# FNet mixing and a quick-GELU block on one core: another order of j for the first transfers, rounding of the weights moved behind the copies, one weight row turned by a transfer, output in runs of 256 bytes with the last group in halves

One core of a Trainium2 chip. The metric is the device time of one launch in microseconds (us); lower is better. PE is the matrix engine (TensorE), DVE VectorE, ACT ScalarE, POOL GpSimd and SP SyncE; loads and stores are issued by SP and ACT, each on a queue of its own. "pa", "psw" and the like are the kernel's names for PSUM banks, and groups of instructions are called by them.

## The reference, cut to what matters

```python
def reference(x, w_in, w_out):            # x 8 x 3008 x 256, w_in 256 x 2048, w_out 2048 x 256
    X = np.fft.fft(np.fft.fft(x, axis=1), axis=2).real.astype(np.float32)
    h = X.reshape(8 * 3008, 256) @ w_in
    g = h * (1.0 / (1.0 + np.exp(-1.702 * h)))
    return (g @ w_out).astype(np.float32)
```

## The kernel before

The FFT over 3008 = 47 x 64 rows is done in two stages of matmuls, with symmetric rows folded on each other first. Between the stages the data goes through DRAM: `spill` writes it to Td, `fill` reads it back. The FFT over 256 columns is folded into w_in (`fold_w`, PSUM name psw; the result is wcs). The weights come as pairs of 32-bit words and are rounded by the kernel, in eight chunks (four of w_in, four of w_out): `bounds` is one operation on POOL (m) and three on ACT (g, r, r), `rounded` three on DVE (m, a, a) and one add on POOL (wst or wo). The long part is 384 steps: `hidden` (pa, pb), `rows` (DVE), `activate` (ACT), `product` (po). For the first sequence all of the preparation stands on the way:

```python
    nc.scalar.dma_start(out=w0, in_=tab1[:, 0:n0 + 1])
    load_first(0, 4, nc.sync)
    load_first(4, 4, nc.scalar)
    load_first(8, 8, nc.sync)
    nc.scalar.dma_start(out=small[:], in_=tab2)
    load_in(0, nc.scalar)
    load_in(1, nc.sync)
    load_out(0, nc.sync)
    warm(10)                                   # matmuls on ones, to keep the clock up
    ...
    for k in range(8):
        if k < 7:
            fold_first(k + 1)
        else:
            bounds(("in", 0))                  # ACT: 3 operations ahead of the last copy
        mix_first(k)                           # 8 matmuls and one copy out of PSUM on ACT
        if k % 4 == 3:
            spill(0, 2 * k - 6, 2 * k + 2, (nc.sync, nc.scalar if k == 7 else nc.sync))
    fill(0, 0, 4)
    round_in(0)
    finish_in(0)
    warm(4)
    bounds(("in", 1))
    fold_w(0)
    fill(0, 4, NG)
    load_out(1, nc.sync)
    rotate(0, 0, 4, nc.scalar.copy)
    stage2(0, 0)
    round_in(1)
    ...                                        # cut
    def nyquist_weights(n):                    # row 0 of wcs[1] turned into a column by matmuls
        ps = bank("psa")
        for f in range(4 * n, 4 * n + 4):
            nc.tensor.matmul(ps[:, f:f + 1], lhsT=wcs[1][0:1, f * 128:(f + 1) * 128], rhs=ones[:, 0:1],
                             start=True, stop=True)
        nc.scalar.activation(af2[:, 4 * n:4 * n + 4], ps[:, 4 * n:4 * n + 4], ACTF.Copy, scale=2.0)
```

Of the kernel before, what the change touches and what calls it, by code (L numbers as in the profile page):

```python
# [34 lines left out]
NA, NB = 47, 64  # L35
# [70 lines left out]
def kernel(ctx: ExitStack, tc, x, w_in, w_out, tab1, tab2, out):  # L106
# [20 lines left out]
    Xr = [nc.dram_tensor(f"Xr{b}", (NA, NJ - 1, D), F32, kind="Internal").ap() for b in range(B)]  # L127
# [27 lines left out]
    def turn(b):  # L155

        for m0, m1 in ((NJ + 1, NJ + 17), (NJ + 17, NB)):
            n = m1 - m0
            nc.sync.dma_start(out=view(Xr[b], (m0 - NJ - 1) * D, [D, n], [(NJ - 1) * D, NA], [1, D]),
                              in_=view(x[b], ((NA - 1) * NB + m0) * D, [D, n], [-NB * D, NA], [1, D]))  # L160

    def load_x(b):

        for r in range(2):
            for p0, p1 in PIECES:
                t, src = xt[64 * r + p0:64 * r + p1], x[b].rearrange("(p j) d -> p j d", j=NB)[p0:p1]
                rev = Xr[b][p0:p1]
                both = [16 * D, 2], [1, 8 * D]
                nc.sync.dma_start(out=t[:, 0:16, :].rearrange("p (c i) d -> p c (i d)", c=2), in_=free(src, 8 * r * D, *both))

                if r:
                    nc.sync.dma_start(out=t[:, 16:32, :].rearrange("p (c i) d -> p c (i d)", c=2),
                                      in_=free(rev, (8 - 8 * r) * D, *both))
                    continue
                nc.sync.dma_start(out=t[:, 16:24, :], in_=rev[:, 8:16, :])
                nc.sync.dma_start(out=t[:, 24:31, :], in_=rev[:, 24:31, :])
                nc.sync.dma_start(out=t[:, 31, :], in_=src[:, NJ, :])
# [24 lines left out]
    def mix1(b, m):  # L202

        ps = [bank("ps1") for _ in range(2)]
        for i in (2 * m, 2 * m + 1):
            for r in range(2):
                for c in range(2):
                    rows, o = slice(64 * r, 64 * r + NA), ps[r][64 * c:64 * c + 64, i % 2 * D:(i % 2 + 1) * D]
                    jj = 16 * c + 8 * r + i
                    if jj:  # L210
                        nc.tensor.matmul(o, lhsT=mat(w1, jj, rows), rhs=xt[rows, 31 - (8 * c + i), :], start=True, stop=True)  # L211
                        continue
# [5 lines left out]
        for r in range(2):  # L218
            q = 8 * r + 2 * m
            nc.scalar.copy(xt[:, q:q + 2, :].rearrange("p j d -> p (j d)"), ps[r][:])  # L220
# [5 lines left out]
    def load_first(lo, n, eng):  # L226
        for p0, p1 in PIECES:
            m = p1 - p0
            both = [16 * D, 2], [1, n * D]
            eng.dma_start(out=free(xt[p0:p1], lo * D, *both), in_=view(x, (NB * p0 + lo) * D, [NB * D, m], *both))  # L230
            for c in range(2):
                a = 16 * c + lo
                t, src = xt[NA + p0:NA + p1], NB * p0 * D
                if a == 0:
                    eng.dma_start(out=t[:, 0, :], in_=view(x, src + NJ * D, [NB * D, m], [1, D]))
                z, a = a + n, max(a, 1)
                eng.dma_start(out=t[:, a:z, :], in_=view(x, src + (NB - a) * D, [NB * D, m], [-D, z - a], [1, D]))

    def fold_first(k):

        t, e = xt[0:2 * NA], room[k % 4][0:2 * NA]

        def src(at, *last):
            return free(t, 2 * k * D + at, [16 * D, 2], [D, 2], list(last))

        def dst(at, *last):
            return free(e, at, [2 * D, 2], [D, 2], list(last))

        nc.scalar.copy(dst(0, H, 2), src(0, H, 2))
        for at, op in ((1, ALU.add), (H + 1, ALU.subtract)):  # L250
            nc.vector.tensor_tensor(dst(at, 1, H - 1), src(1, 1, H - 1), src(D - 1, -1, H - 1), op=op)

    def mix_first(k):

        ps, e = bank("ps1"), room[k % 4]
        for i in range(2):
            for even in range(2):
                for c in range(2):
                    jj, (c0, c1) = 16 * c + 2 * k + i, (0, H + 1) if even else (H + 1, D)
                    w, n = (w0o, jj) if jj and not even else (w0, jj or ENDS[1 - even])  # L260
                    nc.tensor.matmul(ps[64 * c:64 * c + 64, i * D + c0:i * D + c1], lhsT=mat(w, n, slice(0, 128)),  # L261
                                     rhs=e[:, 2 * c + i, c0:c1], start=True, stop=True)
# [13 lines left out]
    def spill(b, q0=0, q1=16, engines=(nc.sync, nc.sync)):  # L276

        for c, eng in enumerate(engines):
            eng.dma_start(out=view(Td[b], (16 * c + q0) * D, [NJ * D, NM], [1, (q1 - q0) * D]),
                          in_=xt[64 * c:64 * c + NM, q0:q1, :].rearrange("p q d -> p (q d)"))  # L280
# [51 lines left out]
    def load_out(n, eng):  # L332
        t = raw["out", n] = cv.tile([128, 1024, 2], U32, tag="raw", bufs=3, name="raw")
        eng.dma_start(out=t[:].rearrange("p (f n) w -> p f (n w)", f=4),
                      in_=w_out[4 * n * 128:(4 * n + 4) * 128, :].bitcast(U32).rearrange("(f p) n -> p f n", p=128))
# [21 lines left out]
    def rounded(out, key):  # L357
# [10 lines left out]
        return lambda: nc.gpsimd.tensor_tensor(out.bitcast(U32), a[:], r[:], op=ALU.add)  # L368
# [4 lines left out]
    def round_in(n):  # L373
        wst[n] = op.tile([128, 2, 512], F32, tag="os", name="wst")
        last["in", n] = rounded(wst[n][:].rearrange("p i f -> p (i f)"), ("in", n))

    def round_out(n):
        ps = slice(2 * n, 2 * n + 2)
        last["out", n] = rounded(wo[:, ps].rearrange("p f q n -> p (f q n)"), ("out", n))
# [14 lines left out]
    def fold_w(n):  # L394
        for cs in range(2):
# [3 lines left out]
            nc.scalar.copy(wcs[cs][:, n * 512:(n + 1) * 512], ps[:])  # L399

    def nyquist_weights(n):
        ps = bank("psa")
        for f in range(4 * n, 4 * n + 4):
            nc.tensor.matmul(ps[:, f:f + 1], lhsT=wcs[1][0:1, f * 128:(f + 1) * 128], rhs=ones[:, 0:1],  # L404
                             start=True, stop=True)
        nc.scalar.activation(af2[:, 4 * n:4 * n + 4], ps[:, 4 * n:4 * n + 4], ACTF.Copy, scale=2.0)
# [96 lines left out]
    def combine(t):  # L503
# [5 lines left out]
        o = op.tile([128, 4, 256], F32, tag="os", name="os")  # L509
        if t < NP:  # L510
            for half in range(2):
                nc.vector.transpose(o[:, 2 * half:2 * half + 2, :].rearrange("p i n -> p (i n)"),
                                    pot[half][:].rearrange("p i n -> p (i n)"))
        else:
            c = cv.tile([128, 4, 256], F32, tag="m", name="c")
            if n < 256:
                nc.gpsimd.memset(c[:, :, n:], 0.0)
            (_, m6), (m2, m7), (m5, m3), (m4, _) = ((pot[q][:, 0, :n], pot[q][:, 1, :n]) for q in range(4))
            u2, u3, u4 = (op.tile([128, 256], F32, tag=f"u{q}", bufs=1, name=f"u{q}")[:, :n] for q in (1, 2, 3))
            c1 = pot["c"][:, :n]  # L520
            c11, c12, c21, c22 = (c[:, q, :n] for q in range(4))
            for out_, i0, i1, how in ((u2, c1, m6, ALU.add), (c11, c1, m2, ALU.add), (u3, u2, m7, ALU.add),
                                      (u4, u2, m5, ALU.add), (c12, u4, m3, ALU.add), (c22, u3, m5, ALU.add),
                                      (c21, u3, m4, ALU.subtract)):
                nc.vector.tensor_tensor(out_, i0, i1, op=how)
            for half in range(2):
                nc.vector.transpose(*(x[:, 2 * half:2 * half + 2, :].rearrange("p i n -> p (i n)") for x in (o, c)))
        store(b, blk, hh, o, n)

    def store(b, blk, hh, o, n):  # L530
# [161 lines left out]
```

## Time and profile before

| | before |
|---|---|
| time, median of the runs beside the changed kernel | 1942.39 us |
| span of the profiled run | 1939.2 us |
| first pa (regular work begins) | 49.63 us |
| first step of width 225 ("step 8") | 102.85 us |
| last matmul ends | 1931.08 us |

These four points cut the span into four pieces: the start (to the first pa), the stretch (first pa to step 8, in which the other weight chunks are prepared beside the first eight steps), the steady part (step 8 to PE's last matmul) and the end. They are read from the timeline of PE: the first line with pa, the first pa line of shape 128x225, and the last line. The prediction shows the first and the last of them; this is step 8 (a line of a timeline has: start, length, engine, line of the kernel, operation, result <- operands, shapes, how many in the group, and in brackets the engine's wait ahead of it and what ended it):

```profile
102.85 0.92 PE L429 MATMUL pa<-pq,wcs 128*128 128x225 f32 x4
```

### The profile page before, as it was taken

The page shows a single profiled execution, that of the slowest core. Times are in us where ns is not written, and L with a number is a line of the kernel's source. Part 1 is how long each engine was busy: PE and PEld are TensorE (multiplying, and loading weights), DVE is VectorE, ACT ScalarE, POOL GpSimd, SP SyncE. Part 2 cuts the span into 40 slices and gives each one's busy share as a digit, 9 for nine tenths or more (in the row PEclk, how much of TensorE's full clock was granted, in tenths as well). Part 3 has the DMA queues.
Part 4 walks back from the last instruction along what each step waited for, and adds up shares of the span by engine and source line. Part 5 has one row for each costly group of instructions (what it writes and reads, how often), then busy time and mean ns, then how long its engine had stood idle before and what let it go on. Part 6 is the DMA issues. An engine that isn't in the chain of part 4 may idle for free.

```text
span 1939.2 us, 29813 instructions
## 1 busy us (share of the span) xinstructions
PE 1908.7 (98%) x10730; PEld 1673.0 (86%) x10730; DVE 1409.5 (73%) x2924; ACT 671.6 (35%) x927; POOL 756.3 (39%) x1045
## 2 busy tenths in 40 slices
PE   6999999999999999999999999999999999999998
PEld 3698888988889888898889888898888988889887
DVE  3867777777778767876777677777776777778766
ACT  3633333333333333333333333333333333333332
POOL 1465223642246322463225522254223642223222
PEclk8999999999999999999999999999999999999999
DMA  8820451227202372134521353222721223202201
GB/s 214 219 51 10 87 84 15 48 46 120 17 12 52 52 112 17 16 53 77 81 21 30 55 90 51 25 48 43 109 28 15 17 46 57 18 12 24 19 12 22
DMA packets 242389, 103.11 MB, mean 53 GB/s; under 512 B 207779, under 2 KB 232099, under 8 KB 238982
## 3 DMA queue, kind: packets, MB, share of 16 engines
q1 hardware_dynamic: 238880, 97.53, 32.2%
q10 hardware_dynamic: 3363, 3.69, 0.7%
q8 instruction: 85, 1.39, 0.3%
q14 instruction: 61, 0.50, 0.1%
HBM read 57.91 MB, written 47.67 MB: 54 GB/s over the span
## 4 chain that ended last, share of the span: by engine, by line
PE 96%; DMA 2%; ACT 1%; DVE 0%; SPq 0%; issue 0%; DVEq 0%; ACTq 0%
PE po L496 59%; PE pa L429 17%; PE pb L429 17%; PE ps L211 1%; PE ps L304 1%; DMA xt<-in_x_dram 1%; DMA raw<-in_moe_w_in_dram 1%; PE psw L398 0%; PE ps L215 0%; DMA Td<-xt 0%; PE ps L261 0%; ACT g L346 0%; PE psa L404 0%; ACT wcs L399 0%; ACT r L353 0%
## 5 line engine op out<-in xcount | busy, mean ns | idle before, releaser
L470 POOL TENSOR_TENSOR s<-h 128x256 f32<-128x256 f32 (+1 forms) x376 | 270.3, 719 | 1093.4 <-ACT h L458 1028.5
L496 PE MATMUL po<-s,wt 128*128 128x256 f32 (+1 forms) x2256 | 599.7, 375 | 0.0
L433 ACT COPY v<-pa 128x512 f32<-128x512 f32 (+1 forms) x384 | 222.0, 578 | 1065.1 <-PE pa L429 1065.1
L443 DVE TENSOR_TENSOR h<-v,pb 128x512 f32<-128x512 f32 (+1 forms) x384 | 259.0, 675 | 402.5 <-PE pb L429 395.1
L496 PEld LDWEIGHTS po<-s,wt 128*128 128x128 f32 x2256 | 428.6, 190 | 48.4
L496 PE MATMUL po<-h,wo 128*128 128x256 f32 (+1 forms) x1632 | 469.6, 375 | 0.0
L458 ACT ACTIVATE h<-h 128x1024 f32<-128x1024 f32 (+1 forms) x384 | 400.8, 1044 | 16.9 <-DVE h L453 15.3
L429 PE MATMUL pa<-pq,wcs 128*128 128x256 f32 (+1 forms) x1536 | 394.8, 379 | 1.2 <-DVE pq L310 1.2
L429 PE MATMUL pb<-pq,wcs 128*128 128x256 f32 (+1 forms) x1536 | 388.6, 375 | 0.0
L496 PEld LDWEIGHTS po<-h,wo 128*128 128x128 f32 x1632 | 310.1, 190 | 35.5
L446 DVE SCALAR_TENSOR_TENSOR dif<-nb,af,pb 128x256 f32<-128x256 f32 (+1 forms) x768 | 328.3, 469 | 3.7 <-ACT nb L322 1.9
L429 PEld LDWEIGHTS pa<-pq,wcs 128*128 128x128 f32 x1536 | 286.9, 190 | 48.2 <-issue 9.6
L429 PEld LDWEIGHTS pb<-pq,wcs 128*128 128x128 f32 x1536 | 292.3, 190 | 33.6 <-DVE dif L446 0.3
L471 POOL TENSOR_TENSOR s<-h 128x256 f32<-128x256 f32 (+1 forms) x376 | 276.7, 736 | 0.0
L453 DVE TENSOR_TENSOR h<-pa,dif 128x512 f32<-128x512 f32 (+1 forms) x448 | 265.4, 604 | 13.2
L496 PE MATMUL po<-s,wo 128*128 128x256 f32 (+1 forms) x752 | 220.3, 375 | 0.0
L496 PE MATMUL po<-h,wt 128*128 128x256 f32 (+1 forms) x752 | 220.3, 375 | 0.0
L474 DVE TENSOR_TENSOR s<-h,s 128x256 f32<-128x256 f32 (+1 forms) x376 | 200.7, 534 | 12.9
L473 DVE TENSOR_TENSOR s<-s,h 128x256 f32<-128x256 f32 (+1 forms) x376 | 180.5, 480 | 4.3 <-POOL s L470 4.3
L496 PEld LDWEIGHTS po<-s,wo 128*128 128x128 f32 x752 | 142.9, 190 | 16.1
L496 PEld LDWEIGHTS po<-h,wt 128*128 128x128 f32 x752 | 142.9, 190 | 16.1
L197 POOL TENSOR_TENSOR xt<-xt 111x510 f32<-111x510 f32 x56 | 74.1, 1323 | 4.4
(62 smaller groups left out, 697.8 us busy)
## 6 DMA issues: line engine op xcount, KB each, us to landing
out_dram<-os SPq DMA_DIRECT2D x568, 32.0 KB
Td<-xt SPq DMA_DIRECT2D x14, 768.0 KB
t<-Td SPq DMA_DIRECT2D x7, 1536.0 KB
xt<-in_x_dram SPq DMA_DIRECT2D x15, 512.0 KB
nb<-pq SPq DMA_DIRECT2D x23, 256.0 KB
out_dram<-os SPq DMA_DIRECT2D x192, 28.0 KB
Xr<-in_x_dram SPq DMA_DIRECT2D x7, 752.0 KB
Xr<-in_x_dram SPq DMA_DIRECT2D x7, 705.0 KB
```

The source lines that it names most:

```text
L197: eng.tensor_tensor(low, low, free(t, up + D - 1, [-D, 2], [-1, D - 1]), op=ALU.add)
L429: nc.tensor.matmul(ps[:, i * 256:i * 256 + n], lhsT=wcs[cs][:, f * 128:(f + 1) * 128], rhs=pq[:, cs, ks], start=True, stop=True)
L433: nc.scalar.copy(two(v[:], n), two(pa[:], n))
L443: nc.vector.tensor_tensor(two(h[:], n), two(v[:], n), two(pb[:], n), op=ALU.add)
L446: nc.vector.scalar_tensor_tensor(dif[:, i * 256:i * 256 + n], nb[:, ks], af2[:, f:f + 1], pb[:, i * 256:i * 256 + n], op0=ALU.mult, op1=AL ...
L453: nc.vector.tensor_tensor(free(h[:], 512 + at + m - 1, [256, 2], [RUN, blocks], [-1, m]), *ins, op=ALU.add)
L458: nc.scalar.activation(g, g, ACTF.Gelu_apprx_sigmoid)
L470: eng.tensor_tensor(s1, a21, a22, op=ALU.add)
L471: eng.tensor_tensor(s3, a11, a21, op=ALU.subtract)
L473: eng.tensor_tensor(s2, s1, a11, op=ALU.subtract)
L474: eng.tensor_tensor(s4, a12, s2, op=ALU.subtract)
L496: nc.tensor.matmul(pot[q][:, i, :n], lhsT=lhs, rhs=rhs, start=(p == 0 and i == 0 and f == 0), stop=(p == NP - 1), skip_group_check=True)
```

## The change

The intent: fewer transfers for the first sequence, in an order in which four neighbouring j make one unit of work, with the weights behind them; the last copies out of PSUM ahead of the rounding; no small matmuls to turn one row of the folded weights; half as many output packets and issues, and the last group's first half stored while the second is summed. The diff, cut:

```diff
-    load_first(0, 4, nc.sync)
-    load_first(4, 4, nc.scalar)
-    load_first(8, 8, nc.sync)
+    both = nc.sync, nc.scalar
+    load_first(0, 8, (nc.sync, nc.sync))
+    load_first(8, 20, both)                    # forward rows on SP's queue, reversed rows on ACT's
+    load_first(20, 32, both)
     nc.scalar.dma_start(out=small[:], in_=tab2)
-    load_in(0, nc.scalar)
+    load_in(0, nc.sync)
     load_in(1, nc.sync)
     load_out(0, nc.sync)
-    warm(10)
+    warm(6)
 ...
         if k < 7:
             fold_first(k + 1)
-        else:
-            bounds(("in", 0))
         mix_first(k)
-        if k % 4 == 3:
-            spill(0, 2 * k - 6, 2 * k + 2, (nc.sync, nc.scalar if k == 7 else nc.sync))
+        if k in (3, 5, 7):
+            spill(0, 0 if k == 3 else 2 * k - 2, 2 * k + 2, both if k == 7 else (nc.sync, nc.sync))
     fill(0, 0, 4)
+    bounds(("in", 0))
     round_in(0)
 ...                                            # fold_w: the row, and wcs read with a stride of 4
-    def nyquist_weights(n): ...
+        row = cv.tile([1, 512], F32, tag="e", name="row")
+        nc.scalar.activation(row[:], ps[0:1, :], ACTF.Copy, scale=2.0)
+        nc.scalar.dma_start(out=af2[:, 4 * n:4 * n + 4], in_=row[:])
 ...                                            # round_out: the columns in another order, two adds on POOL
+            return [(free(out, dh * H, [2 * H, 4], [32, 4], [1, 32]),
+                     [free(t, 32 * dh, [2 * H, 4], [64, 4], [1, 32]) for t in ins]) for dh in range(2)]
 ...                                            # the end
+            if t == len(steps) - 1 and out_ is c12:
+                turned(0, c[:])
+        for half in (1,) if t == len(steps) - 1 else (0, 1):
+            turned(half, c[:, 2 * half:])
 ...                                            # store: 4 transfers of 256-byte runs for 8 of 128
-            for i in range(8):
+        for q in range(4):
```

Cut: the other indices of j in the matmuls, `load_x`, `turn`, `spill` (pieces of 1 KB) and `load_out`, which follow from the new orders.

## The prediction

> **What bounds the kernel now.** I read the page first: how busy each engine is, and the 40 slices.
>
> ```profile
> PE 1908.7 (98%) x10730; PEld 1673.0 (86%) x10730; DVE 1409.5 (73%) x2924; ACT 671.6 (35%) x927; POOL 756.3 (39%) x1045
> PE   6999999999999999999999999999999999999998
> DMA  8820451227202372134521353222721223202201
> ```
>
> TensorE works 98% of the span; only its first and last slices are not full. Next the table of busy time by window.
>
> ```profile
> 20.00:30.00 10.00, 2.09 (x26) 1.88 (x24) 2.91 (x5) 1.20 (x4) 1.09 (x1) 0.80 1.07 244
> 70.00:80.00 10.00, 8.43 (x33) 5.74 (x34) 9.65 (x12) 8.00 (x11) 4.31 (x3) 1.00 1.01 306
> 300.00:500.00 200.00, 200.00 (x1170) 176.72 (x1169) 147.90 (x311) 68.60 (x96) 83.44 (x118) 1.00 0.34 55
> 1920.00:1940.00 20.00, 11.09 (x52) 9.42 (x50) 7.27 (x16) 1.43 (x2) 2.73 (x4) 0.85 0.17 27
> ```
>
> Columns: window, its length, busy time of PE, weight load, DVE, ACT and POOL with counts, granted clock, DMA share, GB/s. From 100 to 1920 us every window shows PE busy for all of its length. So nothing done to DMA, DVE, ACT or POOL there can shorten it; what can shrink is the start (0 to 100 us) and the tail. The timeline of PE shows the start.
>
> ```profile
> 15.23 5.38 PE L261 MATMUL ps<-e,wt 128*64 128x127 f32 x64 [2.93 <-issue]
> 28.52 5.80 PE L261 MATMUL ps<-e,wt 128*64 128x127 f32 x64 [7.91 <-DVE e L251]
> 46.98 0.36 PE L291 MATMUL psr<-t,small 128*128 128x4 f32 x2 [2.24 <-DMA t<-Td]
> 49.63 1.85 PE L429 MATMUL pa<-pq,wcs 128*128 128x256 f32 x4 [1.21 <-DVE pq L310]
> 61.33 1.05 PE L404 MATMUL psa<-ones,wcs 1*128 1x1 f32 x8 [0.77 <-ACT wcs L399]
> 70.89 3.70 PE L398 MATMUL psw<-wst,small 128*128 128x512 f32 x8 [1.41 <-DVE h L453]
> ```
>
> Regular work begins at 49.63 us. Before it the transform of the first sequence waits twice for x: PE has nothing from 20.6 to 28.5. Then comes the way through DRAM. The full chain of waits, asked for the first 110 us, gives its length.
>
> ```profile
> 15.93 11.04 DMA xt<-in_x_dram
> 34.11 1.05 ACT g L346
> 37.80 5.02 DMA Td<-xt
> 44.62 11.83 DMA raw<-in_moe_w_in_dram
> ```
>
> The last x transfer was issued at 15.93 and landed at 26.97. ACT then put 3.1 us of rounding of the weights (L346, L353, L354: 34.01 to 37.21 in ACT's timeline) ahead of the last copy out of PSUM, at 37.21; the write to Td could leave only at 37.80. So the start is set by the order of transfers and of ACT's work, not by PE.
>
> The tail, from the timeline of the end:
>
> ```profile
> 1930.49 0.59 PE L496 MATMUL po<-h,wt 128*128 128x256 f32 x2
> 1932.15 1.30 DVE L527 STREAM_TRANSPOSE os<-c 128x512 f32<-128x512 f32 x2
> 1932.88 3.83 SPq L544 DMA_DIRECT2D out_dram<-os  x8
> 1932.88 3.94 ACTq L544 DMA_DIRECT2D out_dram<-os  x8
> ```
>
> PE ends at 1931.1. Eight issues on each of two queues take 3.9 us, 0.48 us each, until 1936.8; the span ends at 1939.2, 2.4 us later.
>
> **What the Trainium skill says.** "DMA: Bandwidth & Descriptors", section "Queues, rings and completion order", says that the queues of SP and ACT are rings on the same 16 engines, served in ring order, with the engine going round-robin between the rings. The trace agrees: in the start DMA is 0.8 to 1.1 busy and a second queue shares the rate. So an earlier x transfer means later weights; the order decides. The same page, "Specifications", gives 512 B as the least size for line rate. The trace has 207,779 of 242,389 packets below that, and yet a DMA share of about a third in the steady part. "TensorE: Matmul & The Clock Gate", section "Part 1: The HAM clock gate (the "warmup" mystery)", says that the array falls to half clock after an idle window of about 3.4 us. The windows of 1 us agree: after the hole before 46.98 the granted clock is 0.50 from 50 to 53 us. I expect that loss to remain.
>
> **The change, part by part.**
>
> *First transfers of x.* Before, each group of folds takes j from two separate halves, so the first half of the work needs two sets of transfers and the second waits for a third, which stands in the queues among the tables and the first weight chunk. After, four neighbouring j belong together, loads are j 0-8, 8-20, 20-32, and the weights come behind. The bytes do not change: x is 3.08 MB, table 0.8 MB. From the windows of 1 us: by 7 us 1.45 MB had moved, 0.65 MB of it x. With only x under way the rate was 181 GB/s (7 to 13.6 us, both queues) and 153 GB/s (22 to 27 us, one queue). The other 2.43 MB of x at 170 GB/s take 14.3 us: x has landed at about 21.5 us instead of 27.0. That saves 5.5 us, but it pushes weights back. Behind x must pass the small table 0.4 MB, three weight chunks of 1.05 MB each and the spills 1.57 MB, before the fill may start. Weights went at about 390 GB/s (27 to 33 us): 3.55 MB take 9.1 us. The spill now has pieces of 1 KB instead of 8 KB. Packets of 1 KB took 46 ns where they ran well and up to twice that elsewhere, so 1536 packets on 16 engines at 55 ns are 5.3 us. Sum: 21.5 + 9.1 + 5.3 = 35.9 us for the end of the spill, 42.8 before. The compute is not behind that: the last three folds (1.25 us of DVE each) and the PE work on them end at about 26.5 us.
>
> *Copies ahead of rounding.* It takes 3.1 us off ACT ahead of the last copy. It is part of the same path: with the old order 26.5 would be 29.6 us, still ahead of the queue. So I do not add it to the sum. The rounding of the first weights (ACT 1.1, DVE 3.1, POOL 2.4) and its fold on PE (3.7) can end by about 37 us, while the fill lands.
>
> *From the fill to regular work.* Fill issued to landed 4.0 us (42.96 to 46.98), landed to the first hidden matmul 2.65 us, neither changed: 35.9 + 4.0 + 2.65 = 42.6, plus 0.5 for issues: 43.1 instead of 49.6. **Gain 6.5 us.**
>
> *One row turned by a transfer.* L404 goes: four groups, 1.13 + 3 x 1.05 = 4.3 us of PE, and 2.1 us that PE waits for the ACT copies ahead of three of them. In their place ACT does one activation of 1x512 (an estimate from its 128x512 copy: 0.6 us) and issues a transfer (about 0.4 us on ACT), which lands about 2 us on. 6.4 us is the most. But between 68.7 and 94.2 us DVE has almost no gap and between 57 and 70 ACT has none; PE waited 1.4 us for DVE at 70.89. Some of what PE saves becomes a wait for them. On the other side weight chunk 2, which held ACT at 56.5 us (6.9 us after regular work began), should come some 2 us earlier relative to it. **Gain 4 us of the 9.7 us** that this stretch (49.63 to 102.85) spends beyond PE's needed 43.5 us (eight hidden steps of 1.73, five products and three folds of 3.45 each, 2 of small things).
>
> *Output.* Runs of 256 B halve the stores' packets, 192,500 to 96,250, and their issues, 16 to 8 per group. In the steady part this saves nothing on PE. At the end the first half is transposed as soon as its two blocks are summed, and its stores leave under the rest of the sums. After the second transpose (still about 1933.5) two issues per queue are left: 0.96 us, then the 2.4 us. 1933.5 + 3.4 = 1936.9 instead of 1939.2. **Gain 2.3 us.**
>
> *Steady part.* Loads in 2 KB pieces, spills in 1 KB pieces, POOL adds in two halves, transposes with another stride: all beside a PE that never waits. **0 us.** Sum: 6.5 + 4 + 2.3 = 12.8 us; 1942.9 - 12.8 = 1930.1.
>
> **Rivals.** First, x is bound by how its rows are read, not by order: the packets from x ran at half the rate of others (153 GB/s alone). Then longer first transfers on both queues might fall below 150 GB/s, x lands near 24 us, and three chunks of weights are still behind it: only some 3 us of the first term come, total about 1934. Against it: with both queues on x the rate was the higher one. Second, ACT and DVE become the bound at 57 to 94 us: the row, its transfer and strided PSUM reads take more than PE's 4.3 us give. Then the second term is 0 and the sum 8.8: 1934. For it: the full timelines of both. Third, the weights arrive early enough for both to run ahead, and all of the 6.4 us plus the late chunk's wait fall away, with x at 19 us: 6.5 + 2.5 + 8 + 2.3 gives 1923.5. Fourth, a store or fold blocks PE in the steady part through a buffer: four 1 KB-piece spills or af rows that come late would show as PE windows under 200; each per cent is 19 us. The DMA share of 0.34 and DVE at 74% speak against it.
>
> **Range and chances.** Rivals one and two together give 1937, the third 1923.5; I take 1924 to 1937 around 1930. A gain over 2% is 39 us: all that the start and the tail hold beyond PE's work is about 6 + 10 + 50 us, so it is nearly ruled out, 0.01. A loss over 2% needs the fourth rival, 0.01.
>
> **What would show it.** In the timeline of PE the first hidden group (pa) should start at 43 us (41 to 46), the last first-transform copy on ACT at about 26 us, no psa group at all; the windows 300 to 500 us still show 200.00; hidden step 8, of width 225, starts about 10 us earlier than 102.85; stores are eight issues at the end, and the span ends about 5.8 us after PE instead of 8.1; packets fall to about 165,000. If the first pa is near 49 the order bought nothing and the DMA queue is the bound; if it is near 43 but step 8 gains no more than 6, ACT or DVE took the rest. I am wrong outright if the steady windows lose or gain PE time.

## The result

| | before | after |
|---|---|---|
| median | 1942.39 us (1941.14 to 1942.97, 4 runs) | 1937.16 us (1936.33 to 1937.51, 4 runs) |
| ratio | | 0.9973, 95% interval 0.9956 to 0.9991 |

A ratio is the mean time of one kernel's fast runs over that of the other's in the same rounds, so not quite the ratio of the medians. The gain is 5.2 us where 12.8 were foretold.

By pieces, from the two profiled runs:

| piece | before | after | gain | foretold |
|---|---|---|---|---|
| start, to the first pa | 49.63 | 49.34 | 0.29 | 6.5 |
| stretch, first pa to step 8 | 53.22 | 50.87 | 2.35 | 4 |
| steady part | 1828.23 | 1828.24 | 0 | 0 |
| end, after the last matmul | 8.12 | 6.25 | 1.87 | 2.3 |
| span | 1939.2 | 1934.7 | 4.5 | 12.8 |

The page of the changed kernel, first the engines, then the DMA packets:

```profile
PE 1903.0 (98%) x10690; PEld 1667.3 (86%) x10690; DVE 1405.5 (73%) x2924; ACT 673.3 (35%) x927; POOL 761.0 (39%) x1049
...
DMA packets 157652, 103.40 MB, mean 53 GB/s; under 512 B 105403, under 2 KB 142011, under 8 KB 156857
```

PE is as busy as before; packets fell by 85,000, and none of that shows in the time, as the windows of the steady part say, of which this is one (columns as in the prediction):

```profile
300.00:500.00 200.00, 200.00 (x1169) 176.73 (x1168) 147.81 (x313) 68.29 (x95) 84.10 (x119) 1.00 0.33 55
```

The timeline of PE in the start of the changed kernel, and its step 8:

```profile
17.48 3.47 PE L244 MATMUL ps<-e,wt 128*64 128x127 f32 x32 [7.89 <-issue]
23.83 7.13 PE L244 MATMUL ps<-e,wt 128*64 128x127 f32 x96 [2.88 <-DVE e L234]
...
39.01 6.41 PE L392 MATMUL psw<-wst,small 128*128 128x512 f32 x8 [4.42 <-POOL wst L354]
...
49.34 1.13 PE L422 MATMUL pa<-pq,wcs 128*128 128x256 f32 x4 [1.25 <-DVE pq L293]
...
100.21 0.92 PE L422 MATMUL pa<-pq,wcs 128*128 128x225 f32 x4
```

Six of the eight units of the first transform (96 of 128 matmuls) come in one group from 23.83 us: the second and the third set of x landed together. Then PE waits 4.42 us for the rounded weights, and the fold of them takes 6.41 us where the same eight matmuls took 3.70 before. The chain of waits (start, length, what) says the same:

```profile
11.88 10.33 DMA xt<-in_x_dram
...
31.98 1.16 ACT g L329
...
39.01 6.42 PE psw L392 x8
```

The transfers of Td and t, the way through DRAM, are not in it any more; the rounding and the fold of the first weight chunk are. A window shows why the fold is slow; the third number from the right is the granted clock, as a share of full speed:

```profile
40.00:44.00 4.00, 4.00 (x6) 1.69 (x5) 0.00 (x0) 0.59 (x1) 0.02 (x1) 0.50 0.92 302
```

The end, from the timeline:

```profile
1927.86 0.59 PE L489 MATMUL po<-h,wt 128*128 128x256 f32 x2
...
1928.97 0.71 DVE L506 STREAM_TRANSPOSE os<-c 128x512 f32<-128x512 f32 x1
1929.60 0.71 DVE L523 TENSOR_TENSOR c<-u,po 128x256 f32<-128x256 f32 x2
1929.71 2.21 SPq L541 DMA_DIRECT2D out_dram<-os  x4
1929.71 2.28 ACTq L541 DMA_DIRECT2D out_dram<-os  x4
1930.35 0.71 DVE L506 STREAM_TRANSPOSE os<-c 128x512 f32<-128x512 f32 x1
```

The first half's stores are issued under the last sums, as meant.

### The profile page after: what moved, and what is told of

Read it like the earlier page. It is cut to its first block, busy times and chain, and to the rows that moved or that the text cites. A ratio compares the mean times of both kernels' runs of the same rounds, so it can differ in the third digit from the quotient of the medians.

```text
span 1934.7 us, 29225 instructions
## 1 busy us (share of the span) xinstructions
PE 1903.0 (98%) x10690; PEld 1667.3 (86%) x10690; DVE 1405.5 (73%) x2924; ACT 673.3 (35%) x927; POOL 761.0 (39%) x1049
## 2 busy tenths in 40 slices
DMA packets 157652, 103.40 MB, mean 53 GB/s; under 512 B 105403, under 2 KB 142011, under 8 KB 156857
## 3 DMA queue, kind: packets, MB, share of 16 engines
q8 instruction: 85, 1.39, 0.3%
## 4 chain that ended last, share of the span: by engine, by line
PE 96%; DMA 1%; POOL 1%; issue 1%; DVE 1%; ACT 0%; ACTq 0%; SPq 0%; DVEq 0%; POOLq 0%
PE po L489 59%; PE pa L422 17%; PE pb L422 17%; PE ps L205 1%; PE ps L287 1%; DMA xt<-in_x_dram 1%; PE psw L392 1%; PE ps L244 0%; POOL wo L354 0%; PE ps L209 0%; POOL wst L354 0%; POOL m L330 0%; DVE a L350 0%; DVE m L347 0%; DVE os L506 0%
```

## The experiments

All outputs are right. Each ratio is against the kernel before, in the same rounds. "Half-clock loss" is worked out from windows of 1 us between 34 and 104 us: the sum of PE's busy time times (1 - granted clock), ahead of the first pa / in the stretch. It is busy time lost, and a part of it may lie in what would else be a wait.

| run | first pa | stretch | half-clock loss | end | median | ratio (95%) |
|---|---|---|---|---|---|---|
| before | 49.63 | 53.22 | 0.02 / 1.65 | 8.12 | 1942.39 | 1 |
| after | 49.34 | 50.87 | 2.75 / 0 | 6.25 | 1937.16 | 0.9973 (0.9956-0.9991) |
| e1_warm | 47.06 | 50.90 | 0 / 0 | 6.18 | 1934.67 | 0.9966 (0.9954-0.9979) |
| e2_round_first | 45.11 | 54.33 | 0.52 / 5.71 | 6.21 | 1935.40 | 0.9965 (0.9952-0.9977) |
| e3_rings | 47.84 | 54.08 | 1.39 / 5.12 | 6.25 | 1937.86 | 0.9980 (0.9967-0.9994) |
| e3b_short | 48.86 | 50.89 | 2.55 / 0 | 6.32 | 1936.86 | 0.9975 (0.9963-0.9988) |
| e4_nyq | 47.36 | 52.70 | 1.47 / 0 | 6.49 | 1937.38 | 0.9976 (0.9964-0.9989) |
| e5_out | 50.46 | 50.44 | 2.94 / 0 | 7.94 | 1939.16 | 0.9982 (0.9969-0.9994) |
| e7_tail | 49.61 | 54.06 | 1.56 / 5.12 | 6.70 | 1940.67 | 0.9989 (0.9976-1.0001) |
| e9_two_a | 49.62 | 53.99 | 1.55 / 5.12 | 6.23 | 1936.90 | 0.9970 (0.9956-0.9983) |
| e10_all | 45.55 | 52.00 | 0 / 1.70 | 6.19 | 1934.58 | 0.9959 (0.9946-0.9971) |
| e11_add_first | 49.67 | 52.57 | 2.61 / 1.58 | 6.22 | 1938.83 | 0.9981 (0.9967-0.9994) |
| e12_no_flush | 45.67 | 47.66 | 0 / 0 | 6.54 | 1929.84 | 0.9938 (0.9924-0.9952) |
| e13_all_add | 45.22 | 52.53 | 0 / 1.58 | 6.30 | 1934.90 | 0.9959 (0.9945-0.9972) |
| e14_warm_nyq | 45.30 | 53.41 | 0 / 1.70 | 6.45 | 1935.95 | 0.9971 (0.9959-0.9984) |
| e15_warm_out | 46.86 | 53.20 | 0 / 5.12 | 7.90 | 1936.31 | 0.9973 (0.9959-0.9987) |
| e16_warm_tail | 47.31 | 50.92 | 0 / 0 | 6.74 | 1936.03 | 0.9971 (0.9958-0.9983) |
| e17_before_warm | 50.53 | 52.83 | 0.43 / 1.71 | 8.10 | 1941.74 | 1.0002 (0.9989-1.0014) |

From step 8 to PE's last matmul every one of these eighteen profiles has 1828.23 to 1828.26 us. Nothing that was done to packets, stores, transposes or loads moved the steady part. The intervals are 0.0012 to 0.0018 to each side, some 2.5 us, as wide as most of the effects; and the kernel before had medians of 1942.39 beside the changed kernel and of 1941.74, 1941.99, 1941.98 and 1941.36 in the four sets of runs that follow (e1 to e3b; e4, e5, e9, e10; e7, e11 to e13; e14 to e17). So where medians are within some 2.5 us of each other, a verdict below rests on the pieces of the profile.

A profile is one execution, and the start scatters. In e17_before_warm and in the kernel before, the code ahead of the edit is the same, and yet the last of the first transform's matmuls end at 35.48 us in the one and at 34.32 in the other: a difference of about 1 us in the start, between two profiles, may be scatter. Every run lists its mean granted clock, and a run that stands well above the others of its build has the lowest (e9_two_a: 1940.34 us at 0.991, against 1936.08 to 1937.17 at 0.994 to 0.996). The profiles of e2, e7, e9 and e15 are the slowest runs of their builds.

My theory after the result: the first term failed because the rounding of the first weights, not the way through DRAM, sets the start; and because PE, left idle ahead of it, fell to half clock. Rivals: x lands late because of how the queues share it; the way through DRAM is the bound after all. For the second term: a loop of preparing one weight chunk after another sets the pace, so that saved PE time becomes a wait; rivals: PE itself, POOL's two-part adds, the clock.

### e1_warm: no gap ahead of the first weight fold

```diff
-    warm(4)
+    warm(9)
     bounds(("in", 1))
     fold_w(0)
```

> The changed kernel with nine warm-up matmul rounds instead of four ahead of the first weight fold, so that PE has no gap of 4.4 us before it. My theory: the first weight fold sets the start, and it ran at half clock (psw group 6.4 us, granted clock 0.50 from 38 to 44 us). Then psw takes 3.7 us, the first pa starts at 46.9 us (46.4 to 47.6) instead of 49.34, hidden step 8 (width 225) at 97.7 instead of 100.21, time 2.5 us less. Rival one: the stretch after pa is set by when later weights land or by POOL; then pa is at 47 but step 8 stays within 0.7 us of 100.2 and so does the time. Rival two: the fill through DRAM is the bound; then psw gets short and pa stays at 49.3.

```profile
31.29 7.99 PE L257 MATMUL warm<-wcs 128*128 128x512 f32 x18
39.44 3.70 PE L392 MATMUL psw<-wst,small 128*128 128x512 f32 x8 [0.15 <-POOL wst L354]
...
47.06 1.13 PE L422 MATMUL pa<-pq,wcs 128*128 128x256 f32 x4 [1.25 <-DVE pq L293]
```

The fold takes 3.70 us, the first pa comes 2.28 us earlier, step 8 at 97.96 (2.25 earlier), the profiled span is 1932.4 for 1934.7. The theory holds, both rivals fall: the first weight fold was on the path, and 2.3 us of the missing gain were clock. Four of its five runs lie within 0.07 us (1934.67 to 1934.74), closer than any other kernel's.

### e2_round_first: rounding put back ahead of the last copies

```diff
             fold_first(k + 1)
+        else:
+            bounds(("in", 0))
         mix_first(k)
 ...
     fill(0, 0, 4)
-    bounds(("in", 0))
     round_in(0)
```

> The changed kernel with the rounding of the first weight chunk put back ahead of the last copies (the copies-ahead part alone undone). My theory: weights are the bound of the start now, so the earlier rounding gains about 1.3 us on them while the write to Td leaves 3 us later and becomes the bound: first pa at 48.3 to 49.5 against 49.34, time within 0.7 us: the part is worth nothing. Rival (the prediction's picture, the way through DRAM is the bound): the last copy and all after it come 3 us later, first pa at 52.4, time 3 us more.

Both were wrong about the first pa, in the direction that matters: it comes at 45.11 us, 4.2 us earlier. ACT's timeline has the square at 29.41 us for 31.98; the last copy ends at 33.2 for 31.6, and yet the fill is issued at 37.89, 0.84 us sooner than in the changed kernel. So the last copy did not set the spill's landing. That the spill waits behind the weights in the queue fits (the DMA share stays at 0.9 or more until 36 us in both), but is argued and not shown. PE's timeline:

```profile
36.45 3.70 PE L392 MATMUL psw<-wst,small 128*128 128x512 f32 x8 [1.73 <-POOL wst L354]
42.04 0.35 PE L274 MATMUL psr<-t,small 128*128 128x4 f32 x2 [1.89 <-DMA t<-Td]
...
45.11 2.07 PE L422 MATMUL pa<-pq,wcs 128*128 128x256 f32 x4 [1.19 <-DVE pq L293]
```

Now PE waits for t, the fill. But the gap of 1.89 us and the small matmuls of the second stage leave PE so little to do that the first steps run at half clock (2.07 us for 1.13): the half-clock loss in the stretch is 5.71 us and step 8 comes only 0.8 us earlier. "Copies ahead of rounding", the part that I gave 0 us, cost 4.2 us at the first pa; part of this is clock, since against e1_warm (47.06), whose fold took 3.70 us too, it is 1.95 us. What it costs in time is less sure: this build's median is 1.8 us below the changed kernel's, and its fastest run, 1932.90 us at a mean clock of 0.997, 4.3 us below (the profiled one has 0.992).

### e3_rings: queues swapped for the third set of x

```diff
-    load_first(20, 32, both)
+    load_first(20, 32, both[::-1])
```

> The changed kernel with the two queues swapped for the third x transfer (j 20 to 32): forward rows on ACT's queue, reversed on SP's. My theory: in the changed kernel ACT's ring with the 1 KB rows ran dry at 15.0 us and 12 KB packets on SP's ring alone, at about 150 GB/s, set the landing of both the second and the third group (22.4 us), so six folds of DVE (7.3 us) stand behind it. Balanced, the second group lands before 18 us, DVE's last first-fold ends at 26 to 27.5 instead of 29.7, first pa 1.5 to 3 us earlier (46.3 to 47.8). Rival: x is bound by how its rows are read whatever the queue; landing stays at 22 us and first pa within 0.5 us of 49.3.

DVE's folds of the last six units run from 21.91 to 29.17 us, in the changed kernel from 22.40 to 29.66: the rival. The first pa at 47.84 is due to the clock (psw 5.09 us), and half clock in the stretch takes it back. The theory that the split between the queues keeps the second set late finds no support. One profile says little here, though: in e1_warm, with the queues as in the changed kernel, the second and third set are folded from 20.79 and 25.47 us.

### e3b_short: forward rows of x in packets of 1 KB

```diff
-            engines[0].dma_start(out=xt[p0:p1, lo:hi, :].rearrange("p j d -> p (j d)"),
-                                 in_=view(x, src + lo * D, [NB * D, n], [1, (hi - lo) * D]))
+            for o in range(2):
+                ev = [2 * D, (hi - lo) // 2], [1, D]
+                engines[0].dma_start(out=free(xt[p0:p1], (lo + o) * D, *ev),
+                                     in_=view(x, src + (lo + o) * D, [NB * D, n], *ev))
```

> The changed kernel with the forward rows of the first x transfers in packets of 1 KB (even and odd j in two transfers each) instead of 8 and 12 KB. If long packets from x are the slow ones (12 KB took 0.9 to 1.6 us each, 1 KB 46 to 100 ns), the rate while x is alone rises from 150 to above 180 GB/s, x lands at 20 us or before and the last fold ends 2 us earlier. Rival: the rate belongs to the rows of x and not to packet length; then x lands at 22 us or later, since there are twelve times as many packets, and the time is the same or up to 1 us more.

DVE's timeline has the three sets at 13.08, 19.81 and 24.73 us (in e1_warm, with the long packets, 15.98, 20.79 and 25.47; in the changed kernel 16.09 and 22.40). The first and second come 1 to 3 us sooner, the last almost as late as elsewhere, and the time is the same (ratio 0.9975 and 0.9973). Long packets are not what holds x back as a whole: from 7 to 18 us it came at 166 to 187 GB/s here and at 167 to 176 in the changed kernel, while weights ran at some 400 GB/s right behind (25 to 32 us). What in the rows of x is slow was not found.

### e4_nyq and e14_warm_nyq: the turned row undone

```diff
-        row = cv.tile([1, 512], F32, tag="e", name="row")
-        nc.scalar.activation(row[:], ps[0:1, :], ACTF.Copy, scale=2.0)
-        nc.scalar.dma_start(out=af2[:, 4 * n:4 * n + 4], in_=row[:])
+    def nyquist_weights(n): ...                # as before, called at t = 0 and after each fold_w
```

> The changed kernel with the turned row undone alone: small matmuls (psa) and their copy in place of the activation and the transfer of the row. Psa costs PE 4.3 us again. My theory: the prediction's full saving did not come since PE waits for POOL and DVE in that stretch (3.6 us for the weight adds of POOL in the changed kernel), so psa fills waits: first pa about 1 us earlier than 49.34 (no row and no transfer on ACT ahead of the copy of t), step 8 at 100.5 to 102.5 against 100.21, time 0.3 to 2.3 us more. Rival: PE is the bound and all comes back: step 8 at 103.5 to 105, time 4 us more.

The first pa comes 1.98 us earlier, of which 1.28 us are the wait for the copy of t, which stood on ACT behind the row and its transfer, and the rest is a psw of 5.16 us for 6.41 that starts 0.52 us later. The stretch gets 1.83 us longer. Step 8 at 100.06 is 0.15 us earlier than with the row turned, a little below what I gave. Since the clock was in it, the same was run in the kernel without a gap:

> The kernel with nine warm-up rounds (full clock all the way, median 1934.67), with the turned row undone alone. By the stretches seen so far: psa adds 1.8 us between first pa and step 8, the missing row and transfer on ACT give back 1.3 us before pa: pa at 45.6 to 46.1, step 8 at 98 to 99 against 97.96, time 0.2 to 1 us more. The prediction's rival (PE the bound, all of 4 us): step 8 at 101 or later, time 3 to 4 us more.

Against e1_warm the first pa is 1.76 us earlier, the stretch 2.51 us longer with 1.70 us of half-clock loss in it, the span 1.0 us longer and the median 1.3 us more. The turned row is worth about 1 us at most, not 4; it may be nothing, since e1_warm has no half-clock loss to set against those 1.70 us. Psa's 4.3 us of PE and 2.1 us of waits go, and what comes in their place is this (waits of PE in the changed kernel):

```profile
PE psw L392 <- POOL wst L354: 8.1, 3, 4.4
...
PE pb L422 <- DVE dif L439: 1.6, 1, 1.6
...
PE ps L287 <- ACT t L275: 1.3, 1, 1.3
```

3.6 of the 8.1 us lie after the first pa; before there was none of these there (its 3.1 us of that kind lay ahead of pa). The row's transfer, which the prediction let land in about 2 us, took up to 4.4 (issued at 91.07 us, DVE waits for it until 95.50), but PE was full there.

### e5_out and e15_warm_out: the whole output part undone

```diff
-            return [(free(out, dh * H, [2 * H, 4], [32, 4], [1, 32]), ...) for dh in range(2)]
+        last["out", n] = rounded(lambda *ins: [(out, ins)], ("out", n))      # one add on POOL
 ...                                            # combine and store as before: 128-byte runs, no halves
```

> The changed kernel with the output part undone as a whole (runs of 128 B, no halves at the end, one add of POOL for a chunk of w_out). My theory: the adds of POOL in two halves take 3.5 us for 2.4 and stand on the path of 60 to 90 us; undone, step 8 comes 1 to 2.5 us earlier (97.7 to 99.2 against 100.21) and the end, after PE's last matmul, takes 8.1 us instead of 6.25; time within 1 us of the changed kernel. Rival: POOL is beside the path, step 8 stays at 100.2, and the time is 1.9 us more. In the windows 300 to 900 us PE stays at 200.00 with twice the output packets under both.

The stretch gets 0.43 us shorter and the end 1.69 us longer; the time is 2.0 us more. The rival was right: POOL's longer adds (the pair spans 3.5 us for 2.4 in three of four chunks) are nearly all beside the path. With twice the output packets, PE's windows stay full and the steady part is the same to 0.02 us.

> The kernel with nine warm-up rounds, with the whole output part undone. End 1.7 to 1.9 us longer (7.9 to 8.1 us), POOL's single add gives back at most 0.6 us in the stretch: time 1.2 to 1.9 us more. If the two-part add is on the path after all, step 8 comes 1 us or more earlier and the time is less than 1 us more.

The end is 7.90 us and the median 1.6 us above e1_warm, as foretold. But its profiled run had half clock from 47.6 to 57.9 us, with no gap of PE above 1.25 us ahead of it, so its stretch says nothing.

### e7_tail and e16_warm_tail: only the halves undone

```diff
-            if t == len(steps) - 1 and out_ is c12:
-                turned(0, c[:])
-        for half in (1,) if t == len(steps) - 1 else (0, 1):
+        for half in (0, 1):
```

> The changed kernel with the last group not in halves; runs of 256 B kept. It splits the 1.9 us that the end got shorter. My theory: of the time from PE's last matmul to the end (8.1 us before, 6.25 after, 7.9 with the whole output part undone), half comes from the halves and half from eight issues instead of sixteen: here 6.8 to 7.4 us, time 0.5 to 1.2 us more. Rival: the halves are all of it: 7.9 us or more; or nothing: 6.3 us.

The end is 6.70 us, just under what I gave: of the 1.69 us between 7.94 and 6.25, the halves are 0.45 and the longer runs with fewer issues 1.24. The time is 3.5 us more, which no change of the last group can explain: its start and stretch have the same code. Their windows beside each other, the changed kernel and then this run:

```profile
52.00:56.00 4.00, 3.04 (x11) 1.93 (x11) 2.78 (x5) 2.40 (x3) 3.15 (x2) 1.00 0.00 0
56.00:60.00 4.00, 3.84 (x11) 1.71 (x9) 3.59 (x4) 3.41 (x6) 0.67 (x2) 1.00 0.62 191
```

```profile
52.00:56.00 4.00, 4.00 (x8) 1.72 (x7) 2.34 (x4) 1.38 (x2) 2.87 (x2) 0.50 0.00 0
56.00:60.00 4.00, 4.00 (x9) 2.52 (x8) 3.90 (x6) 2.81 (x4) 0.57 (x1) 0.50 0.55 163
```

Half clock from 50.5 to 60.7 us in this run, full clock in the other. In the clock records of the trace the stretches at one clock are multiples of 3.413 us (here 3.413, 6.827 and 10.240), so it matters where the thin work of PE from 40 to 50 us falls in these periods: the fold starts at 40.38 us here and at 39.01 in the changed kernel, with the same code ahead of it. All six runs of this build lie at 1939.5 to 1940.9 us with a mean clock of 0.991 to 0.993 (the changed kernel's four: 0.995 to 0.996), so it is a property of the build rather than a scatter; how the edit of the end brings it about is not shown. The profile of e9_two_a has the same half clock from 50.5 to 60.7 us, as one slow run of five. I take up to 3.5 us as what the clock may do to any of these runs with a half-clock loss; this is an estimate from this pair.

> The kernel with nine warm-up rounds, with only the halves of the last group undone. If the 3.5 us that the run without halves lost were clock alone: step 8 at 97.7 to 98.3, end 6.7 us against 6.2, time 0.3 to 0.7 us more. If the halves act in some way on the start: step 8 at 101 or later again.

Step 8 is at 98.23 us, the end 6.74 for 6.18: as the clock theory foretold. The span is 0.8 us above e1_warm; the median is 1.4 us above it, more than the 0.3 to 0.7 that I gave, and this is not explained.

### e9_two_a: two buffers for a

```diff
-        a = cv.tile([128, 1024], U32, tag="a", name="a")
+        a = cv.tile([128, 1024], U32, tag="a", bufs=2, name="a")
```

> The changed kernel with two buffers for the rounding's tile a, so that DVE need not wait for POOL's two adds of the chunk before (DVE waited 3.5 us for them in three times; room for it comes from keeping the row of ones in a free part of another tile). If the wait of DVE for POOL is what the longer adds cost: those waits are gone, step 8 comes 1 to 2 us earlier. Rival: the chain goes through POOL's own time and the single tile m: step 8 within 0.5 us of 100.2.

The waits of DVE for POOL's adds are gone, and PE's waits for wst after the first pa as well, but half clock came over the stretch (5.12 us), and step 8 is at 103.61. The stretch less that loss is 48.9 us for 50.9, which speaks for the first theory, but a loss can't simply be taken off, and the profiled run (1940.34 us) is 3.4 us above the median of its build. The median (1936.90) is that of the changed kernel. Inconclusive.

### e11_add_first: POOL's add ahead of the next clamp

```diff
         at(t, round_out if kind == "out" else round_in, c)
+        at(t, finish_out if kind == "out" else finish_in, c)
         if t + 1 < len(ahead):
             at(t, bounds, ahead[t + 1])
-        at(t + 1, finish_out if kind == "out" else finish_in, c)
```

> The changed kernel with POOL's add of a weight chunk issued before POOL's clamp (m) of the next chunk, not after it. My new theory: from 50 to 90 us a serial loop per weight chunk (ACT and POOL prepare, DVE rounds between two hidden steps, POOL adds, PE folds) sets the pace, so the saved psa went into waits. The add then comes 1.1 us sooner for each chunk: the folds of chunks 2 and 3 start about 1 us earlier, step 8 at 98.5 to 99.7 with a full clock. Rival: the next clamp comes 2.4 to 3.5 us later and DVE waits for it instead: step 8 at 100.2 or later.

The rival: DVE waits for POOL's m six times, 9.3 us in all, where it waited 1.5 us; step 8 at 102.24, the time 1.7 us more. Its stretch has 1.58 us of half-clock loss, so most of the 1.7 us may be clock. The tile m has one buffer and is in the loop; where the add stands only shifts the wait.

### e12_no_flush: one operation less per chunk on ACT and on DVE

```diff
-        nc.scalar.activation(g[:], hi, ACTF.Square)
 ...
-        dve.scalar_tensor_tensor(m[:], g[:], LOW * LOW, m[:], op0=ALU.is_ge, op1=ALU.mult)
```

> The changed kernel without the step that flushes tiny weights (one activation of 1.1 us on ACT and one operation of 1.2 to 2.6 us on DVE per chunk, eight chunks). It is only a probe: right on these inputs, not for all. If the loop of rounding sets the stretch from first pa to step 8 (50.9 us in the changed kernel, 43.5 us of PE work in it), it gets 3 to 6 us shorter: 45 to 48 us, and the first pa comes 1 us earlier too; time 4 to 7 us less. Rival: PE, the clock and the transfers of weights set it: the stretch stays at 50 to 51 us, time at most 1.5 us less.

```profile
45.67 1.13 PE L420 MATMUL pa<-pq,wcs 128*128 128x256 f32 x4 [1.25 <-DVE pq L293]
...
93.33 0.92 PE L420 MATMUL pa<-pq,wcs 128*128 128x225 f32 x4
```

The stretch is 47.66 us, 3.2 us shorter with no clock loss in either of the two stretches, and nothing of PE's own work was changed. The time is 7.3 us less than the changed kernel's. This is the best evidence on the second term: the rounding on ACT and DVE sets the stretch. Which of the two operations does it, and through which wait, was not separated. The first pa moves by 3.7 us, more than the 1 us that I gave, because the shorter wait of PE (2.12 us for 4.42) spares the clock too: psw takes 3.70 us. This is a probe and no version to use, since it gives up tiny weights.

### e10_all and e13_all_add: versions meant to beat both

```diff
+        else:
+            bounds(("in", 0))                  # as in e2_round_first
 ...
-    warm(4)
+    warm(6)
     bounds(("in", 1))
     fold_w(0)
+    warm(2)
 ...
-    rotate(0, 0, 4, nc.scalar.copy)
+    rotate(0, 0, 4)                            # the copy of t on DVE
 ...                                            # and two buffers of a; e13_all_add: adds first as well
```

> A version meant to beat both: the changed kernel with the first rounding put ahead of the last copies, warm-up matmuls (six rounds before the first weight fold, two after it) so that the clock stays full, the first copy of t on DVE in place of ACT, and two buffers of a. If the clock is what took back the 4.2 us of first pa in the run with the rounding first (pa 45.11, but half clock for some 8 us after it): first pa at 44 to 45.3, granted clock 1.00 from 45 us on, step 8 at 94.5 to 97, time 3.5 to 6 us less than the changed kernel. Rival: the weight chunks' own chain (transfer, rounding, adds) sets step 8 whatever pa does: step 8 at 98 or later.

> The combined version (rounding first, warm clock, copy of t on DVE, two buffers of a) with the adds ahead of the next clamp as well. If the loop sets the stretch and the add is in it: step 8 at 96 to 97 against 97.55 in the combined version, time 0.5 to 1.5 us less than it, and 3 to 5 us less than the changed kernel. Rival: as in the run with the adds first alone, the next clamp comes later and step 8 stays at 97.5.

e10_all has the first pa at 45.55 us with full clock until 67.3 us, but step 8 at 97.55: between what I gave and the rival. Its stretch is 52.00 us with 1.70 us of half-clock loss. Its median of 1934.58 us is 2.6 us below the changed kernel's and its ratio of 0.9959 (with e13_all_add's) the best of the legitimate versions, but e1_warm, which changes one number, has a median of 1934.67; with these intervals the two can't be told apart. Both beat both kernels by their medians; the intervals overlap with the changed kernel's. e13_all_add is the same within its interval: the adds first give nothing.

### e17_before_warm: the kernel before, with more warm-up

```diff
-    warm(4)
+    warm(7)
     bounds(("in", 1))
     fold_w(0)
+    warm(2)
```

> The kernel before, with seven warm-up rounds for four ahead of the first weight fold and two after it, so that its own clock loss (granted 0.74 and 0.84 from 48 to 56 us, 1.65 us of busy time) goes. Clock theory: first pa stays at 49.6 within 0.4, step 8 comes 1 to 2 us earlier (100.9 to 101.9), time 1 to 2 us less: part of the change's gain is to be had without it. Rival: that loss lies in waits for ACT and DVE; step 8 at 102.5 or later.

No gain (ratio 1.0002): the first pa comes 0.9 us later and the half clock moves from 49.9-53.3 us to 55.3-58.8 us instead of going. The expectation failed: the waits were filled, and the clock fell all the same, after 3.4 us in which PE was never idle but spent 2.0 us on the one-row and one-column matmuls of psa and psn. Warm-up pays where it fills a wait long enough to drop the clock, as in e1_warm, and nothing else is shown.

## Why the prediction was wrong

The total looks like the prediction's rivals one and two together (1937.6 by its own figures, 1942.9 - 3 - 2.3, where it wrote 1937). That is luck: their pieces would be 3 and 0 us, and 0.29 and 2.35 were measured.

**What held.** The steady part: 0 us, to 0.03 us in eighteen profiles, whatever the packets did. No psa group, four issues per queue at the end, windows at 200.00. Packets fell to 157,652 (about 165,000 foretold). The fourth rival (a steady loss) did not come. The end: 1.87 us for 2.3; the transposes with the new stride take 0.71 us for 0.65, and from the last issue to the end of the span it is 2.7 us for 2.4.

**The first term, 6.5 foretold, 0.29 measured.** x landed at 22.4 us in the changed kernel's profile (21.5 foretold), and at about 25 us in some others. That size was fair. The step that failed is the one after it: "The compute is not behind that: the last three folds (1.25 us of DVE each) and the PE work on them end at about 26.5 us." Since the second set landed with the third, six folds stood behind it, and the last copy ended at 31.6 (at 32.0 in e1_warm, where the third set came alone, at 25.5). And then: "The rounding of the first weights [...] and its fold on PE (3.7) can end by about 37 us, while the fill lands." It ended at 45.4. The rounding, now behind the copies on ACT, began at 31.98, and POOL's result came at 38.96. I had taken the order of ACT's work as free, because before it had cost the other path 3.1 us; e2_round_first shows that the gain of moving it was none (the fill was not later without it) and the cost 4.2 us at the first pa (1.95 us against e1_warm, where the clock was full). With the rounding in its old place, or a shorter one, four profiles (e2_round_first, e10_all, e12_no_flush, e13_all_add) have the first pa at 45.1 to 45.7 us, and in each of them PE waits 0.5 to 1.9 us for the fill last: so the way through DRAM gained about 4.2 us against 49.63, not 6.5, and that is what this part could have given. The rest of the 6.5 was lost ahead of the fill: the sum has the end of the spill at 35.9 us, and e2_round_first issued the fill at 37.9, with the last of x at 25.2 for 21.5; from there on the sum's 4.0 us held (4.1).

**The clock.** "I expect that loss to remain" was wrong in kind. The Trainium skill, "TensorE: Matmul & The Clock Gate", section "Part 1: The HAM clock gate (the "warmup" mystery)", which the prediction named, puts the fall to half clock at one idle window of about 3.4 us. PE's wait ahead of the first weight fold was 3.09 us before and 4.42 us after. The same eight matmuls took 3.70 and 6.41 us. e1_warm, which fills the gap, gets 2.3 us of it back. I had counted the warm-up matmuls on neither side.

But the length of one wait is not what decides here, and the prediction misread its trace when it said that the windows agree: the hole before 46.98 us was 2.24 us long. As said of e7_tail, the stretches at one clock are multiples of 3.413 us. With PE's busy time counted in these periods, the clock falls 19 times between 30 and 104 us in the eighteen profiles. 18 of the falls follow a period in which PE was busy for 1.75 us or less (0.33 in the changed kernel, 1.70 in the kernel before, 1.45 in e15_warm_out); the other is that of e17_before_warm. No other period with more than 1.75 us was followed by a fall, and those with 1.67 to 1.75 went either way. So in these runs a fall goes with little work in one period, however the waits are cut; and where the periods begin differs from profile to profile (one at 34.3 us in the changed kernel, at 34.9 in e3_rings).

**The second term, 4 foretold, 2.35 measured,** and of this only a part is the turned row's. The prediction's third rival and its middle course took psa's 6.4 us as something PE could keep in part; its second rival (ACT and DVE become the bound) was the right one. The turned row undone costs 1 us at most (e14_warm_nyq, which has 1.70 us of half-clock loss, against e1_warm, which has none), because the row and its transfer stand on ACT ahead of the copy of t (1.28 us at the first pa), and because the loop of rounding holds PE (3.2 us come from one operation less per chunk, e12_no_flush). The kernel before had 1.65 us of half-clock loss in its stretch and the changed one none, so some of the 2.35 us is clock as well.

**Open.** Why x comes at about 170 GB/s when weights come at 400: neither packet length nor the split over the queues changed it. Two rivals were not varied: its rows lie 64 KiB apart in DRAM from one partition to the next, and one of its transfers writes 32 or 15 partitions where one of weights writes 128. How much of the 5.2 us is clock: the build without halves shows 3.5 us between two builds with the same start. And the median of e16_warm_tail.

## What to carry to other kernels

When a change moves work from ahead of one path to behind it, time the path that it moves onto as closely as the one it leaves: here the first fold of weights had as little slack as the copies, and the data behind the copies landed no sooner for having them first. Read PE's waits in the start as work missing in a period of the clock, not only as a sum: when one of them grew from 3.1 to 4.4 us, the matmuls behind it took 2.7 us more (1.4 us more in e3_rings, after the same wait), and a few idle-filling matmuls got most of it back. And before comparing builds at the level of a few us, compare their granted clock in the same windows: two builds with the same code there differed by 3.5 us.

## What the Trainium skill lacked or had wrong

- "TensorE: Matmul & The Clock Gate", section "Part 1: The HAM clock gate (the "warmup" mystery)": it gives one busy window of about 3.4 us as enough to come back to full clock. In e7_tail half clock lasted three such windows (50.5 to 60.7 us) with PE busy in all of them, though 2.1 us of the work were the one-row matmuls of psn; in the changed kernel it went after one full window. Its idle window of about 3.4 us is not needed for the fall: e15_warm_out fell to half clock at 47.6 us after a window with PE busy for 1.45 us, between waits of 1.24 and 1.25 us. The page speaks of short idles elsewhere, but no page gives the amount of work in a window below which the clock falls (here some 1.7 of 3.4 us).
- The same page, same section, says that the window runs freely, that the point of change scatters by some 0.5 us, and that one kernel differs from run to run by it. It does not say that all runs of a build can fall on one side: all six runs of e7_tail (1939.5 to 1940.9 us) lie apart from all four of the changed kernel (1936.3 to 1937.5 us), with the same code in the part that differs.
- "DMA: Bandwidth & Descriptors" has a row on the spacing of rows in HBM that begins at 512 KiB, and none for rows 64 KiB apart: x came at 166 to 187 GB/s from 7 to 18 us, in packets of 1, 8 or 12 KB alike, where weights in packets of 4 and 8 KB came at some 400 GB/s. Whether the spacing is the cause is not shown.
